# A sparse attention with a bilinear feed-forward on one core: the last tile's seven products in two token passes, batch 2's V loads behind its query transfers, plain outputs in four half buffers

## The chip, the cores and the metric

The kernel runs on one core of a Trainium2 chip. The core has five engines with a queue of instructions each: PE (TensorE, matrix products into PSUM), DVE (VectorE), ACT (ScalarE), POOL (GpSimd) and SP (SyncE, which here only issues transfers). Transfers between memory and the on-chip SBUF run on 16 DMA engines beside them. PEld is PE's weight load. The metric is the device time of one execution in microseconds (us); the kernel before takes 340.3 us, the median of three runs from 339.74 to 340.78.

## What is computed

q, k and v have 8 batches, 8 heads, 576 tokens and 64 columns. The first four heads attend to the last 32 tokens, the other four to the earlier tokens of the same residue modulo 32. The result goes, token by token, through a bilinear feed-forward.

```python
def _attn_ref(q, k, v):
    scores = scale * np.matmul(q, k.transpose(0, 1, 3, 2))
    rel = pos[:, None] - pos[None, :]
    mask_local = (rel >= 0) & (rel < stride)
    mask_strided = (rel >= 0) & (pos[None, :] % stride == pos[:, None] % stride)
    ...
    attn = attn / (np.sum(attn, axis=-1, keepdims=True) + 1e-09)
    return np.matmul(attn, v).astype(np.float32)

def _moe_ref(x, w_a, w_b, w_out):
    a = x @ w_a
    b = x @ w_b
    return (a * b @ w_out).astype(np.float32)
```

x has 8 x 576 = 4608 rows and 512 columns; w_a and w_b have 1536 columns, the output is 4608 x 512 in float32.

## The kernel before

**Slots.** The feed-forward runs in nine tiles (t) of 512 tokens, and each tile in 16 slots, so that slot i = 16 t + f. In slots 0 to 11 of a tile `ffn_ab` makes 128 of the 1536 hidden columns: four products with w_a, four with w_b (512 tokens wide, 0.216 us each on PE), a copy of the first on ACT (`a_sb`), and the product of both on DVE (`pf`). In the last four slots the tile is multiplied by w_out: in tiles 0 to 2 by `ffn_y`, twelve products of 512 columns for 128 tokens per slot; in tiles 3 to 8 (`FAST_Y`) by `ffn_ys`, which uses seven products of half matrices for eight (Winograd's form of Strassen's scheme). For these `fast_s` adds and subtracts halves of pf on DVE into `ps`, and `fast_w` does so once with the weights.

**Attention between the slots.** All engines follow the program's own order (a schedule by hand). Batch b's attention is cut into steps: S0 to S7 (scores of a head pair and half, exponent on ACT, mask on DVE) and V0 to V7 (product with V, then normalisation). A table names the position of each: 20 is behind slot 20, and 20.5 in the middle of slot 21. Batches 2 to 7 use `step_VT`: PE writes into bank `o`, ACT takes a logarithm and an exponential of the sums (L463, L464), DVE multiplies into `xT` (L468, L470). There is one `o` buffer, so a V step waits until DVE has read the one before. Batch 2's tokens are first used in slot 32, where the last four heads' part (V6 and V7) comes last.

**Loads and transposes.** POOL issues the loads. For batches from 2 on q and k come in the form that DVE's transposes (`step_D`) take: `kl`, `ql` for the local heads and `natk`, `natq` for the strided ones, and SP then issues transfers that put the transposed blocks into `kT` and `qz`. V comes as `vl` (local) and `vs` (strided, per head), with 64 columns of ones beside it that `fill_v` writes. `do(i, ...)` puts such work behind slot i. From slot 14 on POOL first copies one element of that slot's result to `pace`, so that a load leaves no sooner than its slot. In the kernel before batch 2's vl and vs stand at slots 3 and 6, where nothing paces them: POOL reaches them behind the natk and natq of batch 2. Eight transfers of a queue kind can be under way; the ninth waits for the first.

**Outputs.** In tiles 0 to 2 each slot has a `y_sb` tile of its own, two in all, copied by ACT and sent by SP. SP also issues the kT and qz transfers, in program order.

**The last tile** runs the products in the order 3, 4, 1, 2, 5, 6, 7, each for 256 tokens in two quarters of 128, before the next product. Only product 7 is finished quarter by quarter, its second quarter in two pieces of 128 columns. All nine output transfers are SP's (L606).

```python
        for k in "3412567" if tail else "3417526":
            b, lhs, rhs = plan[k]
            ...
            for q in range(2):
                ...
                        if g == FG - 1:
                            if tail and k == "7":
                                y11(dst, q, n)
                            elif q == 1:
                                post(k)
```

Of the kernel before, what the change touches and what calls it, by code (L numbers as in the profile page):

```python
# [30 lines left out]
def kernel(  # L31
# [465 lines left out]
    def step_X(b, c):  # L497
# [19 lines left out]
                 27.5: "V4", 28: "S6", 28.5: "V5", 29: "S7", 29.5: "V6", 30: "V7"}}  # L517
# [69 lines left out]
    def y_plan(t):  # L587

# [5 lines left out]
        bank = {}  # L594
        v = {}

        tail = t == NT - 1
        y = []
        col = lambda j: slice(HN * j, HN * (j + 1))

        def f32t(nm):
            return fsb.tile([128, 2, HN], F32, tag=nm, name=nm, bufs=1)

        def store(i, q, n):
            rows = out[TTOK * t:TTOK * (t + 1), n].rearrange("(q a i s) c -> a s i q c", q=2, i=2, s=16)
            nc.sync.dma_start(out=rows[:, :, i, q], in_=y[i][:, q, n])  # L606

        def store_half(i, n=slice(0, d_model)):
            for q in range(2):
                store(i, q, n)  # L610

        def post(k):
            if k == "3":
                v["a"] = v["w"] = f32t("ya")
                nc.scalar.copy(v["a"], bank["a"])
                y.extend(fsb.tile([128, 2, d_model], F32, tag="y_sb", name="y_sb", bufs=2) for _ in range(2))
                v["y"] = y
            elif k == "4":
                nc.vector.tensor_tensor(v["w"], bank["b"], v["a"], op=ALU.add)
            elif k == "1":  # L620
                v["e"] = f32t("ye")
                nc.vector.tensor_tensor(v["e"], bank["c"], v["w"], op=ALU.add)
            elif k == "7":
                nc.vector.tensor_tensor(v["e"], v["e"], bank["d"], op=ALU.subtract)
            elif k == "2":
                nc.scalar.copy(y[1][:, :, col(0)], bank["b"])  # L626
                if tail:
                    store_half(1, col(0))
                    nc.gpsimd.tensor_tensor(v["w"], v["w"], y[1][:, :, col(0)], op=ALU.subtract)
            elif k == "5":  # L630
                nc.scalar.copy(y[0][:, :, col(1)], bank["a"])
                if tail:
                    store_half(0, col(1))
                    nc.gpsimd.tensor_tensor(v["e"], v["e"], y[0][:, :, col(1)], op=ALU.subtract)
                else:
                    do(16 * t + 15, nc.gpsimd.tensor_tensor, y[0][:, :, col(0)], v["e"], y[0][:, :, col(1)], ALU.subtract)
                    do(16 * t + 18, store_half, 0)
            elif tail:
                nc.vector.tensor_tensor(y[1][:, :, col(1)], bank["c"], v["w"], op=ALU.add)
                store_half(1, col(1))  # L640
            else:
                nc.vector.tensor_tensor(v["w"], bank["c"], v["w"], op=ALU.add)
                do(16 * t + 17, nc.gpsimd.tensor_tensor, y[1][:, :, col(1)], v["w"], y[1][:, :, col(0)], ALU.subtract)
                do(16 * t + 19, store_half, 1)

        def y11(d, q, n):
            nc.vector.tensor_tensor(y[0][:, q, n], v["e"][:, q, n], d, op=ALU.subtract)
            store(0, q, n)

        plan = {"3": ("a", full(0, 0), wsum(0)), "4": ("b", full(1, 1), wsum(1)), "1": ("c", summed(0), wsum(2)),  # L650
                "2": ("b", summed(2), wfull(0, 0)), "5": ("a", summed(1), wfull(1, 1)), "6": ("c", summed(3), wsum(3)),
                "7": ("d", summed(4), wsum(4))}
        for k in "3412567" if tail else "3417526":
            b, lhs, rhs = plan[k]
            new = b not in bank
            if new and not (tail and k == "7"):
                bank[b] = mm_bank([128, 2, HN])
            for q in range(2):
                cuts = (slice(0, HN),)
                if tail and k == "7":  # L660
                    if q == 1:
                        cuts = (slice(0, 128), slice(128, HN))
                        ends = [psum4["o"].tile([128, 2, 512], F32, tag="o", name="end"),
                                pst.tile([128, 2, 512], F32, tag="st", name="end")]
                    else:
                        ends = [mm_bank([128, 1, 512])]
                for z, n in enumerate(cuts):
                    dst = ends[z][:, 0, :n.stop - n.start] if tail and k == "7" else bank[b][:, q, n]
                    for g in range(FG):
                        nc.tensor.matmul(dst, lhsT=lhs(g, q), rhs=rhs(g)[:, n], start=g == 0 and (tail and k == "7" or new and q == 0),  # L670
                                         stop=g == FG - 1, skip_group_check=True)
                        if g == FG - 1:
                            if tail and k == "7":
                                y11(dst, q, n)
                            elif q == 1:
                                post(k)
                        yield v

    def ffn_ys(t, j, mid):
        if j == 0:  # L680
            yst[t] = y_plan(t)
        n = 21 + (6 if (t, j) == (NT - 1, 3) else 0)
        for i in range(n):
            v = next(yst[t])
            if i == n // 2:
# [6 lines left out]
    def ffn_y(t, j, mid):  # L692
        pf = pfs[t]

        c0 = 0
        for z, n in enumerate((256, 128, 128) if (t, j) == (NT - 1, 3) else (d_model,)):
            y = mm_bank([128, n])
            for f in range(FD):
                nc.tensor.matmul(y, lhsT=pf[:, f, 128 * j:128 * (j + 1)], rhs=wo_sb[:, f, c0:c0 + n],  # L699
                                 start=(f == 0), stop=(f == FD - 1))  # L700
                if f == FD // 2 - 1:
                    mid()
            y_sb = fsb.tile([128, n], F32, tag="y_sb", name="y_sb", bufs=2)
            act = t < NT - 1 or (j + z) % 2 == 1
            (nc.scalar.copy if act else nc.vector.tensor_copy)(y_sb, y)
            r0 = TTOK * t + 128 * j
            (nc.scalar if z == 2 else nc.sync).dma_start(out=out[r0:r0 + 128, c0:c0 + n], in_=y_sb)
            c0 += n
# [3 lines left out]
    with tc.manual_schedule(engines={ENG.PE, ENG.SP, ENG.Pool, ENG.DVE, ENG.Activation}):  # L712
# [29 lines left out]
        for nm in ORDER:  # L742
# [10 lines left out]
            elif nm[0] == "G":  # L753
                mask_group(int(nm[1]))
                if nm == "G1":
# [8 lines left out]
                    load_w(4)  # L764
                    for c in range(4):
                        load_wo(c)
                    load_vl(1)
# [31 lines left out]

        for b in range(FIRST_D, B):  # L800
            g0 = 16 * (b - 2)
            if b == FIRST_D:
                for g, fn, *a in ((0, load_qk, b, False), (1, load_qk, b, True), (3, load_vl, b), (6, load_vs, b)):
                    do(g0 + g, fn, *a)
# [6 lines left out]
            gs = {2: (14, 14, 14, 15, 16, 16, 17, 17, 18, 18), 3: (8, 9, 10, 11, 12, 13, 14, 15, 16, 17)}.get(b) or (  # L811
# [12 lines left out]
        for i, t in ((0, vl_buf[0]), (0, vs_buf[0]), (18, vl_buf[1]), (19, vs_buf[1])):  # L824
            do(i, fill_v, t)
# [3 lines left out]
        for t in FAST_Y:  # L829
# [44 lines left out]
```

## Time and profile before

| | us |
|---|---|
| median of three runs | 340.3 (339.74 to 340.78) |
| the profiled execution | 339.19 |
| its span | 337.0 |
| PE, DVE, ACT, POOL busy | 324.1, 251.7, 202.0, 175.2 |
| last product on PE ends | 330.9 |

The span is the time from the first to the last instruction that the profile holds; some 2 us of the execution lie around it. All instants in this text are us from the span's start. The page's groups say what the work is:

```profile
L545 PE MATMUL mm<-xT,wa_sb 128*128 128x512 bf16 (+1 forms) x453 | 108.9, 357 | 1.3 <-DVE xT L470 0.4
L562 ACT COPY a_sb<-mm 128x512 f32<-128x512 f32 x106 | 62.0, 585 | 48.7 <-PE mm L545 46.4
L565 DVE TENSOR_TENSOR pf<-a_sb,mm 128x512 bf16<-128x512 f32 x72 | 48.5, 673 | 21.0 <-PE mm L545 17.9
```

A row reads: line, engine, operation, output <- inputs, shape, count; then busy us and the mean ns of one; then the idle time of the engine just before them and what ended it. Products overlap in PE's pipeline, so their mean is longer than the time each adds.

### The profile page before, as it was taken

How to read it: one execution, taken by the hardware profiler on the slowest of the kernel's cores; microseconds unless marked ns; L12 is line 12 of the kernel's file. 1: busy time of each engine (PE TensorE's matmuls, PEld its weight loads, DVE VectorE, ACT ScalarE, POOL GpSimd, SP SyncE). 2: the span in 40 equal slices, each digit the busy share in tenths (PEclk: the TensorE clock that was granted, in tenths of full speed). 3: DMA queues.
4: the chain of work that ended last, by engine and by line, in shares of the span. 5: the costliest groups of instructions: out<-in, count | busy, mean ns of one | idle time of the engine just before them, and what ended most of it. 6: DMA issues, size and time to landing. Idle time of an engine off the chain costs nothing.

```text
span 337.0 us, 7611 instructions
## 1 busy us (share of the span) xinstructions
PE 324.1 (96%) x2781; PEld 202.1 (60%) x2814; DVE 251.7 (75%) x475; ACT 202.0 (60%) x326; POOL 175.2 (52%) x293
## 2 busy tenths in 40 slices
PE   8999999999989999999999999999999999999992
PEld 6654555445535554556899985558555854674482
DVE  5867566758849984799999999999878744734561
ACT  5663955458757865787577756875778533223320
POOL 8943639899636644665578557844312031312131
PEclk9999999999999999999999999999999999999998
DMA  9999999998989699978898998999023022004004
GB/s 156 148 203 198 202 178 153 196 145 112 133 153 131 122 76 164 126 136 63 85 73 140 165 115 73 136 178 114 20 65 120 2 66 61 1 7 120 0 2 124
DMA packets 102445, 37.60 MB, mean 112 GB/s; under 512 B 77448, under 2 KB 98312, under 8 KB 102408
## 3 DMA queue, kind: packets, MB, share of 16 engines
q0 software_dynamic: 87760, 19.58, 64.7%
q1 hardware_dynamic: 14648, 17.53, 18.1%
q8 instruction: 22, 0.36, 0.4%
q14 instruction: 15, 0.12, 0.1%
HBM read 39.71 MB, written 9.44 MB: 146 GB/s over the span
## 4 chain that ended last, share of the span: by engine, by line
PE 69%; DMA 16%; POOL 8%; issue 2%; DVE 1%; ACT 1%; SPq 0%; ACTq 0%; POOLq 0%; DVEq 0%
PE mm L545 42%; PE mm L670 16%; DMA vl<-in_v_dram 6%; DMA shared<-in_k_dram 3%; PE o L454 3%; DMA wa_sb<-in_moe_w_a_dram 3%; PE st L356 3%; PE mm L699 3%; DMA qz11l<-tq 2%; PE misc L154 2%; POOL natk L201 1%; POOL natq L201 1%; DMA natq<-in_q_dram 1%; POOL vl L110 1%; POOL vs L110 1%
## 5 line engine op out<-in xcount | busy, mean ns | idle before, releaser
L545 PE MATMUL mm<-xT,wa_sb 128*128 128x512 bf16 (+1 forms) x453 | 108.9, 357 | 1.3 <-DVE xT L470 0.4
L545 PE MATMUL mm<-xT,wb_sb 128*128 128x512 bf16 (+1 forms) x463 | 108.5, 357 | 0.3
L562 ACT COPY a_sb<-mm 128x512 f32<-128x512 f32 x106 | 62.0, 585 | 48.7 <-PE mm L545 46.4
L545 PEld LDWEIGHTS <-wb_sb 128*128 128x128 bf16 x480 | 46.4, 98 | 45.0 <-issue 1.3
L842 POOL CAST pace<-pf 1x1 f32<-1x1 bf16 x83 | 29.3, 353 | 82.5 <-DVE pf L565 73.7
L565 DVE TENSOR_TENSOR pf<-a_sb,mm 128x512 bf16<-128x512 f32 x72 | 48.5, 673 | 21.0 <-PE mm L545 17.9
L545 PEld LDWEIGHTS <-wa_sb 128*128 128x128 bf16 x480 | 42.6, 98 | 31.2
L364 ACT ACTIVATE p<-st 128x576 bf16<-128x576 f32 (+1 forms) x64 | 41.6, 650 | 10.7 <-PE st L356 10.0
L463 ACT ACTIVATE xr<-o 64x576 f32<-64x576 f32 x48 | 31.1, 647 | 24.9 <-PE o L454 24.5
L670 PEld LDWEIGHTS <-ps 128*128 128x128 bf16 x366 | 34.5, 98 | 5.3 <-DVE ps L578 1.2
L699 PE MATMUL mm<-wo_sb,pf 128*128 128x512 bf16 x140 | 33.7, 379 | 0.5 <-DMA wo_sb<-in_moe_w_out_dram 0.2
L464 ACT ACTIVATE xr<-xr 64x576 f32<-64x576 f32 x48 | 32.8, 683 | 1.5
L470 DVE TENSOR_TENSOR xT<-o,xr 64x288 bf16<-64x288 f32 x48 | 21.5, 449 | 14.8 <-ACT xr L464 13.9
L567 DVE TENSOR_TENSOR pf<-a_sb,mm 128x512 bf16<-128x512 f32 x34 | 22.9, 674 | 7.6 <-ACT a_sb L562 5.7
L468 DVE TENSOR_TENSOR xT<-o,xr 64x288 bf16<-64x288 f32 x48 | 21.5, 448 | 9.0 <-ACT xr L464 8.3
L670 PE MATMUL mm<-wf,ps 128*128 128x256 bf16 x210 | 26.3, 273 | 0.1
L374 DVE TENSOR_TENSOR p<-p,mask_l 128x576 int16<-128x576 int16 x32 | 19.4, 606 | 7.5 <-ACT p L364 7.5
L234 POOL DMA_DIRECT2D vs<-in_v_dram x24 | 19.5, 816 | 5.4 <-PE st L356 2.8
L699 PEld LDWEIGHTS <-pf 128*128 128x128 bf16 x144 | 12.9, 98 | 13.4 <-issue 0.5
L842 POOL COPY pace<-y_sb 1x1 f32<-1x1 f32 x18 | 3.4, 188 | 33.4 <-ACT y_sb L626 14.8
L210 POOL DMA_DIRECT2D ql<-in_q_dram x24 | 16.0, 665 | 6.6 <-DMA wo_sb<-in_moe_w_out_dram 3.7
L210 POOL DMA_DIRECT2D kl<-in_k_dram x24 | 16.0, 669 | 5.7 <-issue 3.5
(137 smaller groups left out, 480.2 us busy)
## 6 DMA issues: line engine op xcount, KB each, us to landing
out_dram<-y_sb SPq DMA_DIRECT2D x32, 256.0 KB
vl<-in_v_dram POOLq DMA_DIRECT2D x7, 384.0 KB, 8.4
kl<-in_k_dram POOLq DMA_DIRECT2D x24, 72.0 KB, 3.1
ql<-in_q_dram POOLq DMA_DIRECT2D x24, 72.0 KB, 3.1
vs<-in_v_dram POOLq DMA_DIRECT2D x24, 72.0 KB, 5.1
wo_sb<-in_moe_w_out_dram POOLq DMA_DIRECT2D x4, 384.0 KB, 11.2
natk<-in_k_dram POOLq DMA_DIRECT2D x20, 72.0 KB, 3.1
natq<-in_q_dram POOLq DMA_DIRECT2D x20, 72.0 KB, 3.3
```

Source lines behind the costliest of these rows:

```text
L210: nc.gpsimd.dma_start(out=t[32 * h:32 * h + 32], in_=src[b, h].rearrange("(i y) d -> y i d", y=32))
L364: nc.scalar.activation(p[:M, :, :W], st[:M, :, :W], ACT.Exp, scale=scale)
L463: nc.scalar.activation(r, sums, ACT.Ln)
L464: nc.scalar.activation(r, r, ACT.Exp, scale=-1.0)
L468: nc.vector.tensor_mul(dst[:, W * half:W * (half + 1)], o[:64, j, :W], r[:, j])
L545: nc.tensor.matmul(ps_[:, c0:c0 + n], lhsT=w[:, kk, 128 * f:128 * (f + 1)], rhs=xT[:, kk, x0:x0 + n], start=(kk == first and c0 == 0), sto ...
L562: nc.scalar.copy(a_sb, ab[0])
L565: nc.vector.tensor_mul(pf[:, f, :].rearrange("p (i a s) -> p a i s", i=2, s=16), halves(a_sb), halves(ab[1]))
L567: nc.vector.tensor_mul(pf[:, f, :], a_sb, ab[1])
L670: nc.tensor.matmul(dst, lhsT=lhs(g, q), rhs=rhs(g)[:, n], start=g == 0 and (tail and k == "7" or new and q == 0), stop=g == FG - 1, skip_g ...
L699: nc.tensor.matmul(y, lhsT=pf[:, f, 128 * j:128 * (j + 1)], rhs=wo_sb[:, f, c0:c0 + n], start=(f == 0), stop=(f == FD - 1))
L842: nc.gpsimd.tensor_copy(pace, done)
```

## The change

It has four parts.

1. The last tile has a generator of its own, `y_tail`: all seven products for the first quarter of 128 tokens of each half, then all seven for the second. The first quarters are stored in whole rows of 512 columns once they are complete, the second in pieces, two of them from ACT's queue. `fast_s` runs there group by group behind every second slot, its last group between the additions of the first pass, and no element of `ya` is copied to pace.
2. Batch 2's vl moves to slot 16 and its four vs to slots 18 to 21, behind its kl, ql, natk and natq. The `fill_v` of the first buffers move ahead: that of vl before the load of the last w_a and w_b part, that of vs before the first kl. The last weights, w_out and batch 1's vl are issued behind slot 0 rather than in the list before it, in the same order on POOL.
3. Batch 2's transposes move: K's two halves from slot 14 to 13, the second Q half from 15 to 14, the first strided K part from 16 to 15. V7 of batch 2 moves from 30 to 30.5.
4. Plain outputs (tiles 0 to 2) take one tile of two halves per two slots, two such tiles, so four half buffers.

```diff
-                 27.5: "V4", 28: "S6", 28.5: "V5", 29: "S7", 29.5: "V6", 30: "V7"}}
+                 27.5: "V4", 28: "S6", 28.5: "V5", 29: "S7", 29.5: "V6", 30.5: "V7"}}
...
+    def y_store(eng, t, y, i, q, n=slice(0, d_model)):
+        rows = out[TTOK * t:TTOK * (t + 1), n].rearrange("(q a i s) c -> a s i q c", q=2, i=2, s=16)
+        eng.dma_start(out=rows[:, :, i, q], in_=y[i][:, q, n])
...
+    def y_tail(t):
+
+        plan, y = products(t), y_bufs()
+        w, e = f32t("ya"), f32t("ye")
+        v = {"a": w, "y": y}
+        for q in range(2):
+            if q == 0:
+                bank = {x: mm_bank([128, HN]) for x in "abcd"}
+            else:
+                o = psum4["o"].tile([128, 2, 512], F32, tag="o", name="end")
+                st = pst.tile([128, 2, 512], F32, tag="st", name="end")
+                bank = {"a": o[:, 0, :HN], "b": o[:, 1, :HN], "c": st[:, 0, :HN], "d": st[:, 1, :HN]}
+            c21, c12, c22 = y[1][:, q, col(0)], y[0][:, q, col(1)], y[1][:, q, col(1)]
+            wq, eq = w[:, q], e[:, q]
+            seen = set()
+            for k in "3412567":
+                b, lhs, rhs = plan[k]
+                cuts = [(slice(0, HN), bank[b])]
+                if (k, q) == ("7", 1):
+                    cuts = [(slice(0, 128), bank[b][:, :128]), (slice(128, HN), mm_bank([128, 128]))]
+                for n, dst in cuts:
+                    for g in range(FG):
+                        nc.tensor.matmul(dst, lhsT=lhs(g, q), rhs=rhs(g)[:, n], start=g == 0 and b not in seen,
+                                         stop=g == FG - 1, skip_group_check=True)
+                        if g < FG - 1:
+                            yield v
+                    if k == "3":
+                        nc.scalar.copy(wq, bank["a"])
+                    elif k == "4":
+                        nc.vector.tensor_tensor(wq, bank["b"], wq, op=ALU.add)
+                        if q == 0:
+                            fast_s(t, 1, slice(FG - 1, FG))
+                    elif k == "1":
+                        nc.vector.tensor_tensor(eq, bank["c"], wq, op=ALU.add)
+                        if q == 0:
+                            fast_s(t, 2, slice(FG - 1, FG))
+                    elif k == "2":
+                        nc.scalar.copy(c21, bank["b"])
+                        nc.gpsimd.tensor_tensor(wq, wq, c21, op=ALU.subtract)
+                        if q == 1:
+                            y_store(nc.sync, t, y, 1, q, col(0))
+                    elif k == "5":
+                        nc.scalar.copy(c12, bank["a"])
+                        nc.gpsimd.tensor_tensor(eq, eq, c12, op=ALU.subtract)
+                        if q == 1:
+                            y_store(nc.scalar, t, y, 0, q, col(1))
+                    elif k == "6":
+                        nc.vector.tensor_tensor(c22, bank["c"], wq, op=ALU.add)
+                        y_store(nc.sync, t, y, 1, q, col(q) if q else slice(0, d_model))
+                    else:
+                        nc.vector.tensor_tensor(y[0][:, q, n], eq[:, n], dst, op=ALU.subtract)
+                        if q == 0:
+                            y_store(nc.sync, t, y, 0, q)
+                        else:
+                            y_store(nc.scalar if n.start == 0 else nc.sync, t, y, 0, q, n)
+                    yield v
+                seen.add(b)
...
     def ffn_y(t, j, mid):
...
-            y_sb = fsb.tile([128, n], F32, tag="y_sb", name="y_sb", bufs=2)
-            act = t < NT - 1 or (j + z) % 2 == 1
-            (nc.scalar.copy if act else nc.vector.tensor_copy)(y_sb, y)
...
+        if j % 2 == 0:
+            yst[t] = fsb.tile([128, 2, d_model], F32, tag="y_sb", name="y_sb", bufs=2)
+        y_sb = yst[t][:, j % 2]
+        nc.scalar.copy(y_sb, y)
+        r0 = TTOK * t + 128 * j
+        nc.sync.dma_start(out=out[r0:r0 + 128], in_=y_sb)
...
-                    load_w(4)
-                    for c in range(4):
-                        load_wo(c)
-                    load_vl(1)
...
+        do(0, fill_v, vl_buf[0])
+        do(0, load_w, 4)
+        for c in range(4):
+            do(0, load_wo, c)
+        do(0, load_vl, 1)
+        do(0, fill_v, vs_buf[0])
         for b in range(FIRST_D, B):
             g0 = 16 * (b - 2)
             if b == FIRST_D:
-                for g, fn, *a in ((0, load_qk, b, False), (1, load_qk, b, True), (3, load_vl, b), (6, load_vs, b)):
-                    do(g0 + g, fn, *a)
+                do(0, load_qk, b, False)
+                do(1, load_qk, b, True)
+                do(16, load_vl, b)
+                for h in range(HL):
+                    do(18 + h, load_vs, b, (h,))
...
-            gs = {2: (14, 14, 14, 15, 16, 16, 17, 17, 18, 18), 3: (8, 9, 10, 11, 12, 13, 14, 15, 16, 17)}.get(b) or (
+            gs = {2: (13, 13, 14, 14, 15, 16, 17, 17, 18, 18), 3: (8, 9, 10, 11, 12, 13, 14, 15, 16, 17)}.get(b) or (
...
-        for i, t in ((0, vl_buf[0]), (0, vs_buf[0]), (18, vl_buf[1]), (19, vs_buf[1])):
-            do(i, fill_v, t)
+        do(18, fill_v, vl_buf[1])
+        do(19, fill_v, vs_buf[1])
...
-        for t in FAST_Y:
+        for g in range(FG):
+            for n in range(3 if g < FG - 1 else 1):
+                do(16 * (NT - 1) + 2 * g + 1, fast_s, NT - 1, n, slice(g, g + 1))
+        for t in FAST_Y[:-1]:
```

## The prediction

> **What bounds the kernel now.** I read the page's busy shares first, then windows of ten microseconds, then PE's waits, then the timelines of the windows that are not full.
>
> ```profile
> PE 324.1 (96%) x2781; PEld 202.1 (60%) x2814; DVE 251.7 (75%) x475; ACT 202.0 (60%) x326; POOL 175.2 (52%) x293
> ```
>
> PE (TensorE) works 324.1 of 337.0 us, and the change keeps its multiplications. So it can gain only from the 12.9 us in which PE is idle. The windows (columns: window, sum, then busy us of PE, PEld, DVE, ACT and POOL with their counts, granted clock, DMA share, GB/s) say where these lie:
>
> ```profile
> 60.00:70.00 10.00, 9.25 (x47) 4.21 (x49) 7.60 (x12) 3.73 (x7) 8.65 (x15) 1.00 1.90 175
> ...
> 90.00:100.00 10.00, 8.37 (x62) 4.18 (x63) 3.97 (x9) 6.20 (x11) 2.74 (x7) 1.00 1.18 168
> ...
> 330.00:340.00 10.00, 0.90 (x15) 0.71 (x12) 1.22 (x4) 0.00 (x0) 0.23 (x1) 0.72 0.28 90
> ```
>
> 0.75 us are lost at 60 to 70, 1.63 at 90 to 100, and 6.1 after the last product (330.9 to 337.05). The waits name the first two:
>
> ```profile
> PE o L454 <- DVE xT L470: 1.1, 1, 1.1
> PE st L356 <- DMA qz00l<-tq: 0.6, 1, 0.6
> PE mm L545 <- DVE xT L470: 0.4, 1, 0.4
> ```
>
> The timeline of 92 to 99 us shows the middle loss, that of SyncE's (SP) queue the last one:
>
> ```profile
> 92.47 0.65 ACT L463 ACTIVATE xr<-o 64x576 f32<-64x576 f32 x1 [0.60 <-PE o L454]
> 93.15 0.68 ACT L464 ACTIVATE xr<-xr 64x576 f32<-64x576 f32 x1
> 93.86 0.91 DVE L470 TENSOR_TENSOR xT<-o,xr 64x288 bf16<-64x288 f32 x2 [0.89 <-ACT xr L464]
> ...
> 94.84 0.43 PE L454 MATMUL o<-p,vs 72*128 72x72 bf16 x8 [1.11 <-DVE xT L470]
> ...
> 96.86 0.58 ACT L705 COPY y_sb<-mm 128x512 f32<-128x512 f32 x1 [3.03 <-DMA out_dram<-y_sb]
> 97.47 0.65 ACT L463 ACTIVATE xr<-o 64x576 f32<-64x576 f32 x1
> ```
>
> ```profile
> 327.60 6.15 SPq L606 DMA_DIRECT2D out_dram<-y_sb  x9
> 330.66 0.56 DVE L647 TENSOR_TENSOR y_sb<-ye,end 128x128 f32<-128x128 f32 x2
> ```
>
> Nine output transfers leave SP one after another, some 0.65 us apart. The data is complete at 331.22, the ninth issue ends at 333.75.
>
> **The change, part by part.**
>
> *V7 half a slot later, and four half buffers.* V6 of batch 2 runs on PE at 92.01. Its bank is free at 94.77, after two ACT steps and two VectorE (DVE) multiplies. V7 comes six products after V6, so PE waits 1.11 us. At 30.5 six more lie between: without the wait slot 31 starts at 93.56, its first six products (6 x 0.216 = 1.30) end at 94.86, and V7 starts there, 0.1 us after its bank. Behind it, ACT now stands 3.03 us at the copy of slot 30, since each single buffer has to wait for the output two slots back, and that output is queued on SP behind eight query transfers. With four halves the first copy of a pair waits for a tile before; the last of those outputs would be issued at about 65.6 and the copy comes at 93.8. So ACT goes 93.85-94.43 copy, 95.3-96.65 V7's two steps, DVE's xT 96.67-97.6. Slot 32 needs it with its last key part at 96.68 + 1.30 = 98.0; today this product starts at 99.83. Gain 1.83, less 0.1: **1.7 us**. The next wait there has 0.4 us of slack.
>
> *Batch 2's K transposes one slot earlier.* They stand on DVE from 54.4 to 55.8 (2 x 0.71) in front of V1's normalisation, which would end at 56.6 instead of 55.28. V2 needs V1's bank at 56.12: a new PE wait of 0.5 us. But PE then loses the 0.39 us it stands today at 60.01 before X1. Net cost 0.1 to 0.2. The K rows are there: the last kl transfer of that group, issued at 42.69, took 9.9 us and landed at 52.6.
>
> *Fills and V loads.* POOL spends 51.6 to 54.7 on the two fills (1.40 + 1.83), then issues eight natk/natq, vl and four vs:
>
> ```profile
> 59.08 1.45 POOL L222 DMA_DIRECT2D vl<-in_v_dram  x1
> 60.53 3.24 POOL L234 DMA_DIRECT2D vs<-in_v_dram  x4
> ...
> 67.72 0.66 POOL L210 DMA_DIRECT2D ql<-in_q_dram  x1 [0.99 <-DMA vl<-in_v_dram]
> ```
>
> The first fill moves to before wa at 29.34, where POOL waits 1.58 us for a landing: 1.40 fits. The second moves before kl at 38.7; the first kl starts 1.8 us later, but the fourth waits for a landing until 42.69 anyway. Cost 0. If a landing came sooner, up to 0.3 us, as wo_sb has 0.22 us of PE wait at 48.16 already. natk and natq are issued 3 us sooner. The eight query transfers of the first half leave SP at 59.4 to 65.1 instead of 60.67 to 68.57, because the transposes are earlier and the V packets are not beside them. S0, which waits 0.61 us at 69.5, is served: **gain 0.6**.
>
> vl is now issued at the pace of slot 16, whose pf ends at 63.17: POOL 63.4 to 64.9. V0 loads it as weights at 72.66 today, 72.1 then. Landings of vl counted from the issue took 8.4 here, 7.5 at 85.7, 6.7 at 117, 6.6 at 152, 13.0 at 186, 11.2 at 220. I take 7.5, landing at 70.9 with 1.2 us to spare, as nothing but SP's transfers runs beside it; the ends are 6.6 (no wait) and 13.0 (4.3 us of wait). The four vs go between the kl and ql of batch 3 and behind the four rezero fills (4.4 us); the last leaves at about 81, V6 needs it at 90. Behind these on POOL: batch 3's kl of head 3 leaves at 76.7 instead of 75.7 and lands 2.8 to 5 us later; DVE transposes it at about 79.4, so up to 0.5 us of DVE wait, with V3's bank some 0.5 us behind. natk leaves 3.3 us later, the last at about 86.5, for a transpose at 88.6: up to 0.9 us of DVE wait, before which 0.9 us are idle. I take 0.1 for both.
>
> Here a rule speaks against the change. The Trainium skill, "SBUF — State Buffer", on the shared port pair: a DVE operation in a two-port mode[...] locks GpSimd out, so that transfers which POOL issues wait for their descriptors. The trace has the lock: pace (1x1) takes 0.17 us alone, 1.18 at 323.53 beside additions of two SBUF tiles. But vs issues took 0.81 each at 60 to 64 and 0.85, 0.83, 0.81, 0.81 at 85 to 92, with DVE nine tenths busy. By the rule each of four vs and one vl could lose an addition's 0.7 us, an estimated 3.5 in all, taken from the reserve of the loads; by the row 0.1. I take the row.
>
> *The last tile.* PE today: 321.25 to 330.90, with 0.3 us of gap before 325.48, where the addition of the fourth product waits for the pace that reads ya. This pace goes. In two passes: 78 products at 0.109 (24 took 2.62) = 8.52, plus the twelve narrow ones 0.83 (330.07 to 330.90): PE ends at 330.6. The operands hold: pf's last part ends at 322.21, the sums of the last group (0.29, 0.42, 0.42 by the rows for 256 and 512 columns, the first an estimate) at 322.5, 323.6 and 324.5, needed at 323.1, 323.8 and 325.1. The narrower additions (18 for 7) lie in slots where DVE is half busy: 0.
>
> At the end: c12 and its POOL subtraction (half of 1.27) give e at 330.3, the two narrow DVE pieces (0.28) end at 330.63 and 330.97. Half of the tile leaves SP near 326. In the second pass SP issues at 329.0, 330.3 and 331.0, ACT at 329.6 and 330.7. The last transfer today landed 2.77 us after its issue began (333.15 to 335.92) and the program ended 1.12 us later. 331.0 + 2.77 + 1.12 = 334.9 against 337.05: **gain 2.1**. No transfer from ACT is in the trace; its nearest row is SP's, 0.60 to issue and 2.77 to 3.4 to land (the last three), so the ends are 2.3 and 1.5. The skill's page "DMA: Bandwidth & Descriptors", "Issuing engines are not separate DMA queues", holds that issuing from a second engine saves only the sequencer's time, usually small. By that the ACT part is worth one 0.65 at most; by the row the queue of nine is itself the 2.5 us between 331.22 and 333.75. I take the row: what counts is that only one issue remains after the last data.
>
> **Sum.** 1.7 + 0.6 - 0.2 - 0.1 + 2.1 = 4.1 us. The profiled execution took 339.19 (span 337.05 and 2.1 around it): 335.1 after, span 332.9. The median of the runs is 1.1 above that execution, so I expect 336.2.
>
> **Rivals.**
> *A, the V load comes late.* With the 11.2 us of 220 vl lands at 74.6 and V0 waits 2.5: 338.7; with 13.0, 340.5. For: two of six rows. Against: those two ran beside the fast tiles' stores; here one output of 256 KB does. 0.09.
> *B, only the middle counts.* The tail's transfers share their engines, so the last lands as late as ever, or ACT's landing is slow: gain 2.0, 338.3. For: the last landings bunch at 335.2, 335.5, 335.9. Against: half of the data is gone four microseconds sooner. 0.08.
> *C, slower.* The software queue from 63 us: vl sits ahead of all that POOL issues, and POOL waits for the eighth transfer back (as ql at 67.72 does), so a late vl holds vs and kl of batch 3 as well. Each us of landing beyond 8.7 is one of PE; from 13.9 on the time is over 341.3, at 15 it is 342.4. For: 13.4 was seen once, at 37.28. Against: it then stood behind 1.5 MB of weights. 0.07.
> The forecast keeps 0.76. A change that moved nothing is not among them: the issued order differs on POOL, SP and DVE.
>
> **Numbers.** This kernel tells about 0.3% (1.0 us) from no change. Under 339.3 lie the forecast, B and nearly half of A: 0.87; within, the rest of A: 0.05; above, C and a little of A: 0.08. The low end adds the better tail and no small costs, 335.0; the high end goes to A's 11.2 us: 338.9.
>
> **What would show it.** Right: no ACT wait on out_dram at slots 28 to 31, no wait at V7 and S0, vl landing before 72, the last output issued within 0.2 us of the last DVE piece, the span's end 4 us after the last product. Wrong: PE waiting on vl at V0, DVE waiting on kl near 79, or a last landing later than 334.3.

## The result and the profile after

| | before | after |
|---|---|---|
| median of 5 runs, same chip (us) | 340.39 (339.74 to 340.78) | 336.98 (336.72 to 337.51) |
| ratio, 95% interval | | 0.9899 (0.9884 to 0.9915) |
| the profiled execution, its span | 339.19, 337.0 | 336.98, 335.3 |

The change saves 3.4 us by these runs. A second set of runs of the same two kernels gave 0.9920 (0.9886 to 0.9955), a saving of 2.5 us; there the changed kernel took 337.73, where 336.7 to 337.2 had been expected. In four of the sets below (own_banks, single_bufs, v_loads_back and this second one) one run fell into a slower state of the chip, which the medians count and the ratios leave out. The profiled execution of before was 1.2 us quicker than the median of its runs, that of after was not; so the two traces differ by 2.2 us, and it is 2.2 that they can explain.

The page of after has this row of busy shares, and below it stand the same three windows as before the change (columns as in the prediction):

```profile
PE 326.2 (97%) x2814; PEld 201.8 (60%) x2814; DVE 254.7 (76%) x489; ACT 202.8 (60%) x329; POOL 173.4 (52%) x295
```

```profile
60.00:70.00 10.00, 10.00 (x58) 4.77 (x57) 6.92 (x12) 4.71 (x8) 6.51 (x10) 1.00 0.87 120
...
90.00:100.00 10.00, 9.99 (x78) 4.96 (x75) 7.54 (x15) 7.25 (x12) 6.12 (x13) 1.00 1.77 196
...
330.00:340.00 10.00, 0.34 (x7) 0.17 (x3) 0.55 (x2) 0.00 (x0) 0.00 (x0) 0.83 0.15 40
```

Both holes in the middle are closed: PE is busy for 10.00 and 9.99 us where it had 9.25 and 8.37. PE's waits of after say what is there instead (columns: who waits, for what, us in total, times, longest):

```profile
...
PE end L678 <- DVE y_sb L703: 0.6, 1, 0.6
PE o L410 <- DMA vl<-in_v_dram: 0.5, 1, 0.5
PE mm L730 <- DMA wo_sb<-in_moe_w_out_dram: 0.5, 1, 0.5
PE end L678 <- ACT y_sb L693: 0.5, 1, 0.5
PE end L678 <- ACT ya L683: 0.5, 1, 0.5
```

Three of the five are new, and all three stand in the last tile's products (L678).

The first 60 us of a trace differ by when its loads land: slot 16 begins between 59.05 and 60.94 in the traces of this text. So I count from two instants of each trace: the first product of slot 16, and P, the first product of the last tile's w_out part. S0, V0, V6 and V7 are the first products of these steps of batch 2; an issue is counted where it begins.

| us | slot 16 | S0 | V0 | V6 | V7 | P | PE end | last issue | last landing | span end |
|---|---|---|---|---|---|---|---|---|---|---|
| counted from | span start | slot 16 | slot 16 | slot 16 | slot 16 | slot 16 | P | P | P | P |
| before | 60.15 | 9.41 | 12.79 | 31.86 | 34.69 | 261.10 | 9.65 | 11.90 | 14.65 | 15.80 |
| after | 60.17 | 8.63 | 11.77 | 31.28 | 34.12 | 258.66 | 11.51 | 11.87 | 14.74 | 16.46 |

P comes 2.44 us sooner: 1.02 of it is there at V0, 0.44 is lost again between V0 and V6, and 1.86 comes behind V6. From P on nothing is won: PE ends 1.86 us later than it did, the last transfer is issued at the same distance and lands 0.09 later. From the last landing to the end of the execution it is 3.3 us in before (1.15 to the span's end, 2.14 around the span) and 3.4 in after (1.71 and 1.70), so it is the landing that counts, not the span's end. 2.44 - 0.09 - 0.12 = 2.2, the difference of the traces.

### The profile page after: what moved, and what is told of

Read it like the earlier page. It is cut to its first block, busy times and chain, and to the rows that moved or that the text cites. A ratio compares the mean times of both kernels' runs of the same rounds, so it can differ in the third digit from the quotient of the medians.

```text
span 335.3 us, 7662 instructions
## 1 busy us (share of the span) xinstructions
PE 326.2 (97%) x2814; PEld 201.8 (60%) x2814; DVE 254.7 (76%) x489; ACT 202.8 (60%) x329; POOL 173.4 (52%) x295
## 4 chain that ended last, share of the span: by engine, by line
PE 75%; DMA 12%; POOL 7%; DVE 2%; issue 2%; ACT 0%; DVEq 0%; POOLq 0%
PE mm L545 44%; PE mm L650 14%; PE mm L730 7%; DMA vl<-in_v_dram 4%; PE o L454 4%; PE st L356 3%; DMA shared<-in_k_dram 3%; DMA wa_sb<-in_moe_w_a_dram 3%; PE end L678 1%; PE mm L678 1%; POOL shared L195 1%; DMA kl<-in_k_dram 1%; POOL ql L210 1%; DMA natk<-in_k_dram 1%; POOL vl L222 1%
## 5 line engine op out<-in xcount | busy, mean ns | idle before, releaser
L545 PE MATMUL mm<-xT,wb_sb 128*128 128x512 bf16 (+1 forms) x472 | 110.2, 357 | 0.1
L545 PE MATMUL mm<-xT,wa_sb 128*128 128x512 bf16 (+1 forms) x472 | 110.3, 358 | 0.0
L880 POOL CAST pace<-pf 1x1 f32<-1x1 bf16 x84 | 28.4, 339 | 85.1 <-DVE pf L565 73.8
L730 PE MATMUL mm<-wo_sb,pf 128*128 128x512 bf16 x144 | 34.4, 379 | 0.5 <-DMA wo_sb<-in_moe_w_out_dram 0.5
L650 PEld LDWEIGHTS <-ps 128*128 128x128 bf16 x300 | 28.5, 98 | 4.4 <-DVE ps L578 1.2
L650 PE MATMUL mm<-wf,ps 128*128 128x256 bf16 x180 | 22.7, 273 | 0.1
```

Source lines behind the costliest of these rows:

```text
L545: nc.tensor.matmul(ps_[:, c0:c0 + n], lhsT=w[:, kk, 128 * f:128 * (f + 1)], rhs=xT[:, kk, x0:x0 + n], start=(kk == first and c0 == 0), sto ...
L650: nc.tensor.matmul(bank[b][:, q], lhsT=lhs(g, q), rhs=rhs(g), start=new and q == 0 and g == 0, stop=g == FG - 1, skip_group_check=True)
L880: nc.gpsimd.tensor_copy(pace, done)
```

## The experiments

Each diff is against the changed kernel unless it says otherwise. Kernels with the same number under "before" share its runs on one chip.

### Parts alone

*middle_only* is before with everything but the last tile's products; *tail_only* is before with the last tile's products only.

> The kernel before with everything but the new last tile. Theory (the middle is worth the 2.4 us by which slot 32 comes sooner, the tail of the change about 1.0): 2.3 to 2.5 us under the kernel before, 337.9 to 338.1. Rival (the two profiles mislead by 1.2 us, as the profiled execution before lay below its median; the middle is worth more): 3 us or more under it, below 337.4.

> The kernel before with the new last tile alone. Theory (the queue on SP goes, but the waits of the second pass give most of it back): 0 to 1.1 us under the kernel before, 339.3 to 340.4. Rival (the tail brings its predicted 2.1): 338.3. Rival (the waits cost more than the queue gave): above 340.4.

| | median | before | ratio (95%) | slot 16 to P | P to last landing |
|---|---|---|---|---|---|
| middle_only | 337.00 | 339.79 | 0.9913 (0.9896 to 0.9931) | 259.08 | 14.57 |
| tail_only | 340.10 | 339.79 | 1.0012 (0.9985 to 1.0039) | 261.20 | 14.99 |

The middle gives all of the gain. The last tile in two passes gives nothing, and if anything costs some tenths. By the runs middle_only is 2.8 us below before, more than the 2.3 to 2.5 expected; its trace has 2.0 of them at P and 0.1 behind it. Where the rest comes from is not shown.

### Why the last tile gave nothing: two results in one tile

The timeline of after, last tile (columns: start, duration, engine, line, operation, out<-in, count, and in brackets the wait before it and what ended it):

```profile
323.59 7.70 SPq L605 DMA_DIRECT2D out_dram<-y_sb  x5
...
324.78 0.82 PE L678 MATMUL end<-wf,pf 128*128 128x256 bf16 x6 [0.46 <-ACT ya L683]
...
327.46 0.81 PE L678 MATMUL end<-wo_sb,ps 128*128 128x256 bf16 x6 [0.46 <-ACT y_sb L693]
...
329.51 0.49 PE L678 MATMUL end<-wf,ps 128*128 128x128 bf16 x6 [0.58 <-DVE y_sb L703]
...
330.38 0.29 DVE L706 TENSOR_TENSOR y_sb<-ye,mm 128x128 f32<-128x128 f32 x1
```

All three waits are in the second pass. Product 4 waits until ACT has copied product 3, product 5 until ACT has copied product 2, product 7 until DVE has used product 6. None of these reads the bank that the waiting product writes. But in the second pass the banks a and b are the two halves of one tile (o), c and d those of another (st), and each wait names a reader of the other half. *own_banks* gives each result a tile of its own; only the last narrow piece takes the tile o, then free.

```diff
-            if q == 0:
-                bank = {x: mm_bank([128, HN]) for x in "abcd"}
-            else:
-                o = psum4["o"].tile([128, 2, 512], F32, tag="o", name="end")
-                st = pst.tile([128, 2, 512], F32, tag="st", name="end")
-                bank = {"a": o[:, 0, :HN], "b": o[:, 1, :HN], "c": st[:, 0, :HN], "d": st[:, 1, :HN]}
+            bank = {x: mm_bank([128, HN]) for x in "abcd"}
...
-                    cuts = [(slice(0, 128), bank[b][:, :128]), (slice(128, HN), mm_bank([128, 128]))]
+                    cuts = [(slice(0, 128), bank[b][:, :128]), (slice(128, HN), psum4["o"].tile([128, 2, 512], F32, tag="o", name="end")[:, 0, :128])]
```

> The changed kernel with one bank per result in the second pass too (four of the rotating ones), the last piece of 128 columns in the o tile. Theory (one tile over two banks makes PE wait for a reader of the other bank): the waits before products 4, 5 and 7 of the second pass, 0.62 + 0.62 + 0.74 us of gap, go, and the median falls by 1.5 to 2.0 us to 335.0 to 335.5. Rival (ACT and DVE are late with the results, whichever bank holds them): the gaps stay and the median stays within 0.4 us of 337.0.

Measured: 335.59 against 339.79, 0.9868 (0.9846 to 0.9890), a little above the 335.0 to 335.5 expected. Its timeline of the last tile:

```profile
323.59 5.96 SPq L605 DMA_DIRECT2D out_dram<-y_sb  x5
324.81 0.82 PE L673 MATMUL mm<-wf,ps 128*128 128x256 bf16 x6
325.56 1.47 PE L673 MATMUL mm<-wo_sb,ps 128*128 128x256 bf16 x12
326.87 1.15 PE L673 MATMUL mm<-wf,ps 128*128 128x256 bf16 x12
...
328.51 0.28 DVE L701 TENSOR_TENSOR y_sb<-ye,end 128x128 f32<-128x128 f32 x1
```

No product waits; the last DVE piece starts at 328.51 where it was 330.38. PE's end stands 9.53 after P instead of 11.51, and 1.98 is the sum of the three gaps on PE (0.62, 0.62, 0.74, counted from where the next product would have started, 0.109 after the last; the brackets count from the end that the profile models). The landing follows by only 1.27: from 14.74 to 13.47 after P.

### Why the last landing keeps late: half of the DMA engines

In own_banks the last transfer, of 64 KB, lands 3.35 us after its issue begins; in after it took 2.87. In before the last three took 3.4, 3.07 and 2.77. The later the issue, the shorter the landing: that is what a backlog looks like. Here are windows of two microseconds, first at the end of before, then at that of own_banks (the last two columns are the share of the 16 DMA engines that is busy, and GB/s):

```profile
329.00:331.00 2.00, 1.90 (x24) 1.61 (x21) 1.33 (x4) 0.00 (x0) 1.24 (x1) 1.00 0.51 158
331.00:333.00 2.00, 0.00 (x0) 0.00 (x0) 0.22 (x1) 0.00 (x0) 0.00 (x0) 1.00 0.50 161
333.00:335.00 2.00, 0.00 (x0) 0.00 (x0) 0.00 (x0) 0.00 (x0) 0.00 (x0) 0.74 0.53 170
```

```profile
327.00:329.00 2.00, 1.36 (x19) 1.12 (x16) 0.91 (x3) 0.37 (x1) 1.27 (x2) 1.00 0.53 191
329.00:331.00 2.00, 0.00 (x0) 0.00 (x0) 0.00 (x0) 0.00 (x0) 0.00 (x0) 1.00 0.50 150
```

The share stands at one half while transfers are outstanding. The output of the last tile is written as `rows[:, :, i, q]` of a view `(q a i s)` with s = 16, whose outermost dimension a is 8. The Trainium skill, "DMA: Bandwidth & Descriptors", section "Why a DMA increments its semaphore by 16 and not by 1", says in its paragraph on how many engines a transfer uses that the number is the largest, up to 16, that divides the outermost dimension of both sides: 8 here. The *16 kernels* let the last tile's tokens run by 8 in place of 16, so that a is 16; the products and bytes stay as they are:

```diff
-            halves = lambda x: x.rearrange("p (a i s) -> p a i s", i=2, s=16)
-            nc.vector.tensor_mul(pf[:, f, :].rearrange("p (i a s) -> p a i s", i=2, s=16), halves(a_sb), halves(ab[1]))
+            run = 8 if t == NT - 1 else 16
+            halves = lambda x: x.rearrange("p (a i s) -> p a i s", i=2, s=run)
+            nc.vector.tensor_mul(pf[:, f, :].rearrange("p (i a s) -> p a i s", i=2, s=run), halves(a_sb), halves(ab[1]))
...
-        rows = out[TTOK * t:TTOK * (t + 1), n].rearrange("(q a i s) c -> a s i q c", q=2, i=2, s=16)
+        rows = out[TTOK * t:TTOK * (t + 1), n].rearrange("(q a i s) c -> a s i q c", q=2, i=2, s=8 if t == NT - 1 else 16)
```

*own_banks16* is own_banks with it, *before16* is before with it.

> The kernel with one bank per result, and runs of 8 tokens in the last tile. Theory (eight engines bind the end: their packets run without a break from 1 us after the first store until 1.6 us before the end): the backlog goes, the last landing comes 2.3 to 2.8 us after its issue instead of 3.35, and the median falls by 0.6 to 1.0 from 335.6 to 334.6 to 335.0. Rival (landing has a fixed length): within 0.3 us of 335.6.

> The kernel before with the last tile's tokens laid out in runs of 8 instead of 16, so that the outer dimension of an output transfer has 16 steps instead of 8. Nothing else differs. In the kernels so far the output packets of the last tile keep about 8.4 of the 16 DMA engines busy, at 0.08 to 0.09 MB per 0.5 us. Theory (the end is bound by eight engines, an outer dimension of 8 uses no more): up to 16 are busy, the packets end within 1.5 us of the last issue (now 1.6 after its end), and the end comes 0.4 to 1.0 us sooner, 338.8 to 339.4 if the kernel before shows 339.8. Rival (the nine issues on SP bound the end, as the prediction has it): the last issue is still at 12.0 us from the last tile's first product and the end moves less than 0.3 us. Rival (rows of fewer tokens make DVE or the transfers slower): slower than before.

| | median | before | ratio (95%) | last issue | last landing (from P) |
|---|---|---|---|---|---|
| own_banks16 | 334.84 | 340.13 | 0.9838 (0.9803 to 0.9874) | 10.05 | 12.35 |
| before16 | 339.04 | 340.13 | 0.9964 (0.9944 to 0.9985) | 11.71 | 13.75 |

Both medians lie in the ranges expected.

The windows of own_banks16, and behind them one of before16, show the share rise above one half:

```profile
325.00:327.00 2.00, 2.00 (x20) 1.70 (x19) 0.85 (x2) 0.37 (x1) 0.01 (x1) 1.00 0.86 255
327.00:329.00 2.00, 1.48 (x20) 1.24 (x17) 0.91 (x3) 0.37 (x1) 1.40 (x2) 1.00 0.28 73
329.00:331.00 2.00, 0.00 (x0) 0.00 (x0) 0.00 (x0) 0.00 (x0) 0.00 (x0) 1.00 0.72 190
```

```profile
333.00:335.00 2.00, 0.00 (x0) 0.00 (x0) 0.00 (x0) 0.00 (x0) 0.00 (x0) 1.00 0.76 200
```

In own_banks16 it rises to 0.86 and 255 GB/s; the backlog is gone at 327 to 329 (0.28), and the last transfer lands 2.30 after its issue instead of 3.35. In before16 the landing comes 0.90 sooner while the last issue stays (11.71 for 11.90): SP's nine issues are the limit that is left, and in own_banks16, where seven issues are shared with ACT, the landing comes another 1.40 sooner. So before had two limits one on top of the other, the engines first and SP's queue just behind.

No view lists the single DMA engine, but the traces' semaphore events count what takes part in a transfer: each output of the last tile ends in 9 of them in before (81 for nine transfers) and in own_banks (63 for seven), and in 16 in before16 (144) and own_banks16 (112). That fits eight engines with one event more, and sixteen; what the ninth event is no run here shows. The shorter runs also change the order in which a transfer walks the rows of the output. Packets and bytes stay the same, and no run changes the count of engines without that order.

### The middle: half slot and half buffers

*v7_early* puts V7 back to 30; *single_bufs* gives each output of the plain part one of two single buffers again.

```diff
-... 29: "S7", 29.5: "V6", 30.5: "V7"}}
+... 29: "S7", 29.5: "V6", 30: "V7"}}
```

> The changed kernel with V7 of batch 2 back at 30. Theory (V6 to V7 needs 2.8 us of chain, six products give 1.3): PE waits 1.1 to 1.3 us at V7, the four half buffers keep slot 32 free of waiting, and the median rises by 1.0 to 1.3 to 338.0 to 338.3. Rival (the wait of ACT on the output caused both): no wait at V7 and no change, within 0.4 us of 337.0.

```diff
...
-        if j % 2 == 0:
-            yst[t] = fsb.tile([128, 2, d_model], F32, tag="y_sb", name="y_sb", bufs=2)
-        y_sb = yst[t][:, j % 2]
...
+            y_sb = fsb.tile([128, n], F32, tag="y_sb", name="y_sb", bufs=2)
...
```

> The changed kernel with the plain outputs of before, one buffer per slot and two in all. Theory (the wait of ACT on the output blocks V7's two steps behind it): ACT waits 2 to 3 us at a copy of slots 28 to 31, slot 32 waits for xT, and the median rises by 0.8 to 2.0 to 337.8 to 339.0. Rival (V7 at 30.5 alone frees ACT, as its steps now stand elsewhere in ACT's order): within 0.4 us of the changed kernel.

| | median | before | ratio (95%) | V6 (from slot 16) | V6 to P | slot 16 to P |
|---|---|---|---|---|---|---|
| before | | | | 31.86 | 229.24 | 261.10 |
| after | | | | 31.28 | 227.38 | 258.66 |
| v7_early | 338.53 | 339.79 | 0.9954 (0.9936 to 0.9972) | 31.69 | 228.66 | 260.35 |
| single_bufs | 343.40 | 340.13 | 1.0089 (1.0061 to 1.0117) | 32.34 | 233.57 | 265.91 |

With V7 at 30 its wait is back. The timeline of v7_early, V6 and V7:

```profile
91.49 0.42 PE L454 MATMUL o<-p,vs 72*128 72x72 bf16 x8 [0.51 <-DVE xT L470]
...
94.31 0.43 PE L454 MATMUL o<-p,vs 72*128 72x72 bf16 x8 [1.11 <-DVE xT L470]
```

P comes 1.69 later than in the changed kernel, but 0.41 of that is lost before V6, where the moved step plays no part (the next section has its cause). From V6 on it is 1.28. That agrees with the 1.0 to 1.3 expected; the median, 338.53, is just above the 338.0 to 338.3.

With single buffers and V7 at 30.5 the kernel is slower than before. 337.8 to 339.0 had been expected: the wait was foreseen, its length and what follows it were not. The timeline of single_bufs, two lines:

```profile
98.45 0.58 ACT L739 COPY y_sb<-mm 128x512 f32<-128x512 f32 x1 [4.47 <-DMA out_dram<-y_sb]
...
101.42 0.58 PE L545 MATMUL mm<-xT,wa_sb 128*128 128x512 bf16 x1 [3.13 <-DVE xT L470]
```

ACT waits 4.47 us for an output to leave its buffer; V7's two ACT steps stand behind that copy, and PE waits 3.13 for their result at slot 32. Then the windows:

```profile
100.00:105.00 5.00, 3.58 (x14) 1.61 (x14) 3.75 (x7) 3.14 (x6) 3.67 (x8) 0.55 1.30 186
105.00:110.00 5.00, 5.00 (x29) 2.40 (x27) 2.41 (x5) 2.80 (x5) 1.81 (x4) 0.76 0.79 52
110.00:115.00 5.00, 4.95 (x38) 2.71 (x38) 4.78 (x10) 3.73 (x6) 2.93 (x6) 1.00 0.64 97
```

The granted clock (third column from the right) falls to means of 0.55 and 0.76. In the trace's clock record it stands at 0.50 from 100.54 to 107.37, at 1.00 before and behind. From V6 on P is 6.19 later than in the changed kernel. 3.13 of that are the wait; 5.95 us of the half clock lie behind the wait, and at half speed (four products take 1.70 us from 102.71 on, 0.86 elsewhere) 2.98 of them are lost. Together that is 6.11.

So, counted from V6 to P, both parts together bring 1.86. The half slot is 1.28 of it, with the half buffers in place; the half buffers with V7 at 30 are 0.58 (229.24 to 228.66); the half slot without them costs 4.33, the half clock included, since the later V7 then stands behind a blocked copy.

### The middle: transposes and V loads

*v_loads_back* issues batch 2's V loads where before did, *gs_back* restores the schedule of K transposes, *gs_loads_back* does both.

```diff
...
-                do(16, load_vl, b)
-                for h in range(HL):
-                    do(18 + h, load_vs, b, (h,))
+                for g, fn, *a in ((0, load_qk, b, False), (1, load_qk, b, True), (3, load_vl, b), (6, load_vs, b)):
+                    do(g0 + g, fn, *a)
...
-            gs = {2: (13, 13, 14, 14, 15, 16, 17, 17, 18, 18), ...
+            gs = {2: (14, 14, 14, 15, 16, 16, 17, 17, 18, 18), ...
```

> The changed kernel with batch 2's vl and vs back at slots 3 and 6, unpaced. Theory (their packets delay the query transfers from SP and so S0): PE waits up to 0.6 us at S0, less by what the earlier transposes give, and POOL is 3 us ahead at slot 22, which takes 0.4 us off at V3 and V6; the median changes by -0.3 to +0.4. Rival (the loads' place is what brings the 1.0 us at slot 20): the median rises by 0.8 to 1.2.

> The changed kernel with batch 2's transposes in the slots of before, V loads late as changed. Theory (the earlier transposes alone free S0, as moving the V loads back changed nothing): PE waits 0.3 to 0.9 us at S0, and the median rises by 0.3 to 0.9 against the changed kernel of the same call. Rival (either part is enough): no wait at S0 and the same time within 0.3 us, as the query transfers then run without the V packets beside them.

> The changed kernel with both the transposes' slots and the V loads of before. Theory and rival agree that PE waits 0.6 to 1.0 us at S0 here; POOL is ahead for batch 3, which gives 0.2 to 0.4 back. Median 0.3 to 0.8 above the changed kernel of the same call.

| | median | before | ratio (95%) | S0 | V0 | V6 | P (from slot 16) |
|---|---|---|---|---|---|---|---|
| after, second set, with the last two | 337.73 | 340.19 | 0.9920 (0.9886 to 0.9955) | 8.63 | 11.77 | 31.20 | 258.57 |
| v_loads_back | 336.89 | 340.13 | 0.9899 (0.9864 to 0.9934) | 8.63 | 11.77 | 30.84 | 258.22 |
| gs_back | 337.89 | 340.19 | 0.9923 (0.9896 to 0.9950) | 8.63 | 11.77 | 31.83 | 259.20 |
| gs_loads_back | 336.90 | 340.19 | 0.9891 (0.9863 to 0.9919) | 9.40 | 12.60 | 31.67 | 259.05 |

The times of these four can't be told apart; the traces can. S0 loses its wait (9.40 to 8.63) by either edit alone: only with both back does PE wait 0.6 us there again. For gs_back a wait had been expected; the rival, that either edit is enough, was right. gs_loads_back was to be 0.3 to 0.8 slower than the changed kernel of its set and was 0.8 quicker, within the noise. The single wait is not a steady figure: in the four traces with both of the old orders it is 0.6, 0.9, 1.8 and 0.6 us, within S0, and the transfer that lands last is not always the same. V0 tells the two kinds apart: 12.60 to 13.93 from slot 16 in those four, 11.77 in the ten others.

The earlier transposes have a gain of their own, before slot 16. From V1 of batch 1 to slot 16 it is 6.02 or 6.03 us in the five traces with the old transposes and 5.83 in the nine with the new.

And moving the V loads costs on its own. The timeline of after on DVE:

```profile
79.82 0.78 DVE L299 STREAM_TRANSPOSE tk<-kl 128x576 bf16<-128x576 bf16 x1 [0.94 <-DMA kl<-in_k_dram]
89.79 0.71 DVE L304 STREAM_TRANSPOSE tk<-natk 128x512 bf16<-128x512 bf16 x1 [1.31 <-DMA qz10l<-tq]
```

The first line is batch 3's kl, late because a vs issue (76.18 to 77.01) and the vl fill (1.41 from 74.74) stand before its issue on POOL; the fill stood there in before too, the vs issues did not. The second transpose, planned at 88.6 from the trace of before, starts at 89.79. The trace puts that down to a query transfer (qz10l), but natk's last load, issued at 86.16 where it was 83.25 in before, lands at 89.71, just before it. V0 of after is 1.02 us sooner than in before, V6 only 0.58: 0.44 is lost on the way. From V0 to V6 it is 19.06 or 19.07 us in all five traces with the early V loads, and 19.43 to 20.06 in the seven with the late loads and fills and the half buffers (19.51 in after). So the V loads behind the query transfers, one of the change's named parts, bring nothing that the earlier transposes don't bring alone, and cost 0.4 to 1.0.

### A version with both faults mended

*best* is own_banks16 with the two fills of batch 3's V buffers moved from slots 18 and 19 to slot 25, behind POOL's issues of that stretch:

```diff
-        do(18, fill_v, vl_buf[1])
-        do(19, fill_v, vs_buf[1])
+        do(25, fill_v, vl_buf[1])
+        do(25, fill_v, vs_buf[1])
```

> The changed kernel with one bank per result, runs of 8 tokens in the last tile, and the two fills of batch 3's V buffers moved from slots 18 and 19 to 25, behind the loads of batch 3's keys and queries. Theory (POOL's lateness makes DVE wait 0.94 us on kl and 1.31 on natk, and PE 0.2 + 0.15 behind it): both DVE waits go, 0.2 to 0.4 us under the kernel with banks and runs of 8 (334.8), so 334.4 to 334.7. Rival (DVE's waits were covered): 334.8 within 0.2.

Measured: 333.59 against 340.19, 0.9813 (0.9773 to 0.9853), 6.6 us below before. 334.4 to 334.7 had been expected, so it is quicker than the reckoning. In its trace V6 comes at 30.84 and P at 258.21 from slot 16, as in v_loads_back: with the fills out of the way the late V loads cost nothing. The last landing is 12.33 after P. Its page shows PE with 324.4 us in a span of 331.4:

```profile
PE 324.4 (98%) x2814; PEld 201.5 (61%) x2814; DVE 255.0 (77%) x489; ACT 202.3 (61%) x329; POOL 173.6 (52%) x295
```

The step from own_banks16 to best (0.6 us in P) is shown by the traces; the intervals of the two times overlap.

## Why the prediction was right and wrong

**Right in time, wrong in where, and partly by luck.** 336.2 was forecast, 336.98 and, in the second set, 337.73 were measured. But of the gain of 4.1, 2.0 was to come from the middle and 2.1 from the last tile; by the traces the middle gave 2.4 and the last tile -0.1. That is the split of rival B, which had 0.08. Its reason, that the tail's transfers share their engines, is half of what happened.

The forecast's own working was for the profiled execution: 335.1, where 336.98 was measured, 1.9 more. The median came within 0.8 because the 1.1 us by which the runs of before lie above its profiled execution did not return in after. That was luck, and nearly half of the gain that was worked out did not come.

**V7 and half buffers: right.** 1.7 was worked out from the timeline; from V6 to P it is 1.86. (That P moves by 1.69 when V7 is put back looks closer and is chance: 0.41 of it lies before V6.) The four halves had been argued as a condition of it, and single_bufs shows that they are. ACT's copies at slots 28 to 31 no longer wait for an output, as asked for.

**K transposes and S0: nearly right.** A gain of 0.6 at S0 against 0.78 measured (1.02 by V0). The cause was put down to both moves together; either is enough. The price of 0.1 to 0.2 at V2 was a gain of 0.2: PE waits 0.19 at V2 in after, where 0.5 had been reckoned, and the 0.39 before X1 is gone. wo_sb's wait grew from 0.22 to 0.47, inside the 0.3 allowed for the fills.

**V loads: the load right, what stands behind it too small.** vl is issued at 63.8 and lands 7.2 us later, at 71.0 (7.5 and 70.9 forecast), before V0 at 71.94; rivals A and C fell. POOL's lateness was put at 0.1 and is 0.44 in this trace. The working had up to 0.5 us of DVE wait at kl and 0.9 at natk as bounds; the trace has 0.94 and 1.31. I took both as hidden by idle time, and they were not. The rule on the shared port (the Trainium skill, "SBUF — State Buffer") was weighed against the row, and the row held: the four moved vs issues took 0.83 to 0.84 us each, so the lateness is one of order, not of locks. Nor would the page ask for the 3.5 us: in its section "Who interferes with whom", an addition of two SBUF tiles contends with a GpSimd instruction that reads SBUF, as pace does, and it is the two-port modes that hold up transfers.

**The last tile: two steps failed.** The first is "The operands hold. ... PE ends at 330.6", that is 9.35 after P. It is 11.51. I had checked when the operands of each product come, and not when the bank it writes is free in the sense the program waits for: two results in one two-bank tile wait for each other's readers. own_banks, where they don't, ends at 9.53, so the count of products was right to 0.2. DVE's last piece and the last issue move with it, which is why the mark "the last output issued within 0.2 us of the last DVE piece" came true (330.70 after 330.67) and meant nothing.

The second is "331.0 + 2.77", with the 2.77 taken from the last landing of before as if it were the time of a transfer. It was the end of a backlog on a part of the engines; landings of 3.4, 3.07 and 2.77 in a row, all near 335.5, said so, and I had listed that bunching under B. Against the rule that issuing from a second engine is no second queue (the Trainium skill, "DMA: Bandwidth & Descriptors", "Issuing engines are not separate DMA queues") I took the row, SP's nine issues. The row was real (before16 meets it), but it was the second limit: on own_banks the issue comes 1.78 sooner than in before and the landing 1.18. With both faults mended the landing is 2.30 before that of before, counted from P. That it is near the 2.1 of the forecast proves nothing for it: 0.90 is what the shape alone gives in before16, and the forecast had no such term.

**The marks.** The landing "later than 334.3" was too loose as a sign of failure: the last landing came at 333.6 in after, and would have passed even with no gain at the tail, since before's 335.9 less the middle's 2.0 is 333.9. The mark that spoke was the end 4 us after the last product: it came 4.95 after. One of the three signs of being wrong also came true: DVE waited 0.94 on kl at 79.8.

## What to carry to other kernels

When results are put into the free halves of larger accumulator tiles, look for who reads the other half: the program may wait for that reader, though the banks differ. Before a transfer's landing time is used in a sum, look at the DMA share around it: a share that stands still at a fraction with transfers outstanding (here 0.50 to 0.53) points to a backlog, and the outermost dimension of the DRAM side is a thing to vary. A wait that is worth moving by half a slot may need buffers for what then queues in front of it; test such parts both together and apart, and count from the step itself, so that what happens before it stays out of the figure.

## What the runs showed of the hardware

- **The clock in a hole.** In single_bufs PE has nothing to do from 98.29 to 101.42, and the granted clock goes to 0.50 at 100.54, 2.25 us into the hole, for 6.83 us; some 3 us of time were lost by it. The 1.11 us hole in before left it at 1.00. At the kernels' ends it goes to 0.50 between 1.5 us (tail_only) and 5.0 us (middle_only) after the last product. The Trainium skill, "TensorE: Matmul & The Clock Gate", "What's actually happening", gives an idle window of about 3.4 us for the step to half. In these traces such a window need not be wholly idle: in the 3.4 us before the fall PE was still busy for 0.34 of the time in single_bufs, and for 0.00 to 0.38 at the ends of the fourteen traces.
- **An output's shape and its engines.** Outermost dimension 8: share 0.50 to 0.53 and 150 to 191 GB/s in the full windows, 9 semaphore events per transfer; 16: up to 0.86 and 255 GB/s, 16 events, with the same bytes and packets.
- **Issues from ACT.** With the outermost dimension at 8 the first transfer that ACT issued, of 128 KB, held it 1.22 us and the next, of 64 KB, 0.62; with 16 the same two took 0.65 and 0.56. SP's take 0.60 and 0.54 to 0.57 on the same two kernels (after and own_banks16). The first one's landing, 2.8 after its issue began, is like the 2.87 of SP's last.
- **After the last landing** it is 3.2 to 3.5 us to the end of the execution in the traces compared here, while the part of it that lies inside the span goes from 1.15 to 1.72.
